# Stores of the first three output chunks: other shares of their odd rows for the sixteen DMA engines

## The chip, the cores and the metric

The kernel runs on one core of a Trainium2 chip. The metric is the device time of one execution in microseconds (us), the median of three runs. Transfers between the chip's memory (HBM) and the core's on-chip memory run on 16 DMA engines, numbered 0 to 15. A transfer is issued by an engine's instruction stream, here by SyncE's (SP) or by GpSimd's (POOL), and is cut into packets on some or all of the 16 engines.

## The reference

Linear attention, a norm of each row, and a soft mixture of experts on its output, all in float32:

```python
kv = np.einsum('bhsd,bhse->bhde', k, v)
out = np.einsum('bhsd,bhde->bhse', q, kv)
x = out / np.sqrt(np.mean(out * out, axis=-1, keepdims=True) + 1e-06) * g_norm   # then rows of B*S by H*D
logits = x @ phi
d = softmax(logits, axis=0)
slot_input = (d.T @ x).reshape(E, S_per_e, D)
slot_out[e] = np.maximum(slot_input[e] @ w1[e], 0.0) @ w2[e]      # for each of 8 experts
result = softmax(logits, axis=1) @ slot_out.reshape(n_slots, D)
```

q, k and v are 8 batches of 8 heads of 576 by 64; there are 8 experts of 4 slots each, with w1 of 512 by 1024 and w2 of 1024 by 512. The output has 4608 rows of 512.

## The kernel before, in words

The program is a list of instructions that is written out in order; a small planner (`Order`) adds the semaphore waits that data make necessary. TensorE builds kv for each batch, then makes the 36 tiles of the attention's output one after another; ScalarE, VectorE and GpSimd norm them and make logits and exponentials. After the last tile come the experts: `expert_h` reads w1, `expert_y` reads w2, and `output` multiplies the combine weights with the slots' results.

All inputs arrive by large transfers of 128 partitions on SP's queue, in the order in which they are used. The last two are weights: one of 4 MB and, behind it, `load_w("w2", 7)` of 2 MB (line 1001). Their places in the on-chip arena are taken by output chunks afterwards.

The output is made in 12 chunks (`n` from 0 to 11; six for each half of the columns). A chunk is a tile of 128 partitions with 1536 numbers each, so one row of one chunk is 6,144 bytes. ScalarE copies the first half of a chunk from PSUM to the arena, VectorE the second. `OUT_ROWS` groups the chunks for the stores: 0 to 2, 3 to 5, 6 and 7, 8 to 11. The last three groups are one transfer each, of 128 partitions, issued from SP when the last chunk of the group is there; each DMA engine takes eight rows of them.

The chunks 0 to 2 are stored otherwise, by the table `FIRST` (line 56), which is all that the change touches, beside `STEPS` (line 61). An entry reads (issuing engine, first row, step between rows, number of rows, pieces `a`, cuts of a row `c`, first chunk, chunk behind the last one). The entry's rows leave as one transfer as soon as its last chunk is there. The table is laid out for this division: with `a` = 1 and 32 or 64 rows a transfer is spread evenly over all 16 DMA engines; with `a` > 1 and rows uncut (`c` = 1) it is cut over `a` engines, on SP's queue the engines 0 to a - 1, on GpSimd's queue the `a` engines that are next in turn; with `c` = 3 it goes to one engine. GpSimd's turn is meant to start at engine 0 and to move on with each transfer by the number of engines that it used. `step_over(n)` is a tiny transfer of n rows of two runs of 16 bytes, which is there to move the turn on by n engines:

```python
    def step_over(n):
        ends = [x[:n, : 2 * w].rearrange("p (c n) -> p c n", c=2)[:, :, :4] for x, w in ((stepped, 8), (first_in, 64))]
        nc.gpsimd.dma_start(*ends)
```

All its calls write the first n rows of one small tile, `stepped`. The first call stands ahead of the experts (line 984); in `store_first` another follows each transfer of GpSimd's while `STEPS`, read from its end, has a number left:

```python
                getattr(nc, engine).dma_start(dst, src)
                if engine == "gpsimd" and steps:
                    step_over(steps.pop())
```

When an instruction writes where a transfer writes, the planner makes it wait until that transfer has landed (`settle`, line 189). At the end SP waits for all the stores.

Of the kernel before, what the change touches and what calls it, by code (L numbers as in the profile page):

```python
# [53 lines left out]
OUT_ROWS = ((0, 1, 2), (3, 4, 5), (6, 7), (8, 9, 10, 11))  # L54
CHUNK = 4 * 12 * 32
FIRST = (
    ("sync", 1, 4, 30, 5, 1, 0, 1), ("sync", 121, 4, 2, 3, 3, 0, 1),
    ("gpsimd", 1, 4, 24, 2, 1, 1, 2), ("gpsimd", 97, 4, 8, 2, 1, 1, 2),
    ("sync", 3, 4, 32, 1, 1, 0, 2), ("sync", 0, 2, 64, 1, 1, 0, 3), ("sync", 1, 2, 64, 1, 1, 2, 3),
)  # L60
STEPS = (7, 6)
SHARED = (5, 11)
BEHIND = {4: (2, 3), 5: (4, 5, 6, 7)}
HEAD = 144
# [224 lines left out]
def soft_moe_linear_attention(nc, first_in, kv_in, q0_in, q1_in, kv4_in, kv5_in, t3_in, w_in, out):  # L289
# [637 lines left out]

    steps = list(STEPS[::-1])

# [169 lines left out]
```

## Time and profile before

| | |
|---|---|
| median of 3 runs | 171.88 us (171.85 to 172.44) |
| the profiled execution's own time | 171.79 us |
| its span, first to last instruction | 170.5 us |
| granted TensorE clock over the span | 0.978 |
| DMA: packets, bytes, mean rate | 4221, 71.65 MB, 420 GB/s |
| queue of SP, share of the 16 engines' span | 97.8% |
| TensorE, ScalarE, VectorE, GpSimd busy | 88%, 52%, 51%, 35% |

The profile's page and the views of its trace come from one execution; their times are microseconds from the first instruction. The profiled execution took 1.3 us more than its span and lies 0.09 us below the median. The share of a DMA queue is the time of its packets over the time of 16 engines, so 100% means that all sixteen moved data throughout.

### The profile page before, as it was taken

The page shows a single profiled execution, that of the slowest core. Times are in us where ns is not written, and L with a number is a line of the kernel's source. Part 1 is how long each engine was busy: PE and PEld are TensorE (multiplying, and loading weights), DVE is VectorE, ACT ScalarE, POOL GpSimd, SP SyncE. Part 2 cuts the span into 40 slices and gives each one's busy share as a digit, 9 for nine tenths or more (in the row PEclk, how much of TensorE's full clock was granted, in tenths as well). Part 3 has the DMA queues.
Part 4 walks back from the last instruction along what each step waited for, and adds up shares of the span by engine and source line. Part 5 has one row for each costly group of instructions (what it writes and reads, how often), then busy time and mean ns, then how long its engine had stood idle before and what let it go on. Part 6 is the DMA issues. An engine that isn't in the chain of part 4 may idle for free.

```text
span 170.5 us, 4241 instructions
## 1 busy us (share of the span) xinstructions
PE 149.4 (88%) x1836; PEld 104.3 (61%) x1836; DVE 86.8 (51%) x185; ACT 88.8 (52%) x230; POOL 59.6 (35%) x73
## 2 busy tenths in 40 slices
PE   7988698989999899999899998989999989989200
PEld 3467587979778878897688683346656633545000
DVE  1122137284677266762946598833888236318300
ACT  3036467795985886859758874102222134418300
POOL 7000707738367745477382778500000004000000
PEclk9999999999999999999999999999999999999965
DMA  5999999999999999999999999999999999999996
GB/s 181 420 444 418 443 409 438 467 416 451 458 419 417 445 441 423 419 400 467 400 465 392 452 404 425 432 452 406 431 431 442 436 442 392 423 409 444 419 450 288
DMA packets 4221, 71.65 MB, mean 420 GB/s; under 512 B 774, under 2 KB 774, under 8 KB 906
## 3 DMA queue, kind: packets, MB, share of 16 engines
q1 hardware_dynamic: 3850, 71.18, 97.8%
q8 instruction: 14, 0.23, 0.5%
q0 software_dynamic: 352, 0.20, 0.4%
q14 instruction: 5, 0.04, 0.1%
HBM read 61.94 MB, written 9.44 MB: 419 GB/s over the span
## 4 chain that ended last, share of the span: by engine, by line
PE 59%; DMA 14%; ACT 12%; DVE 6%; SPq 2%; issue 1%
PE psum L215 59%; DMA arena<-in_kv_dram 14%; ACT bd L215 3%; ACT sq L215 3%; ACT xall L215 2%; SPq L215 2%; DVE logits L215 1%; DVE ms L215 1%; ACT part L215 1%; ACT arena L215 1%; ACT d L215 1%; DVE part L215 1%; ACT r L215 1%; DVE acc L215 1%; DVE r L215 0%
## 5 line engine op out<-in xcount | busy, mean ns | idle before, releaser
L215 PE MATMUL psum<-bd,arena 128*128 128x192 f32 (+1 forms) x320 | 56.1, 335 | 2.1 <-ACT bd L215 1.5
L215 PEld LDWEIGHTS psum<-bd,arena 128*128 128x128 f32 (+1 forms) x320 | 45.4, 179 | 9.0 <-ACT bd L215 2.8
L215 DVE TENSOR_REDUCE ms<-sq 128x16 f32<-128x1024 f32 (+1 forms) x19 | 22.1, 1162 | 32.7 <-ACT sq L215 32.4
L215 POOL TENSOR_TENSOR part<-part,r 128x512 f32<-128x512 f32 x17 | 17.8, 1047 | 49.8 <-DVE r L215 49.8
L215 POOL TENSOR_TENSOR xall<-xall,r 128x512 f32<-128x512 f32 x34 | 34.7, 1042 | 0.0
L215 ACT ACTIVATE sq<-psum 128x512 f32<-128x512 f32 x36 | 21.5, 597 | 10.9 <-PE psum L215 10.7
L215 PEld LDWEIGHTS psum<-arena 128*64 128x64 f32 (+1 forms) x640 | 18.9, 137 | 8.1 <-DMA arena<-in_kv_dram 3.5
L215 PE MATMUL psum<-arena 128*64 128x64 f32 (+1 forms) x640 | 21.4, 226 | 2.6 <-DMA arena<-in_kv_dram 2.4
L215 ACT COPY xall<-psum 128x512 f32<-128x512 f32 x34 | 20.7, 607 | 0.0
L215 ACT COPY part<-psum 128x256 f32<-128x256 f32 (+1 forms) x38 | 13.6, 359 | 8.6 <-DVE part L215 7.5
L215 DVE TENSOR_REDUCE logits<-part 128x64 f32<-128x512 f32 (+1 forms) x18 | 17.8, 990 | 0.0
L215 PE MATMUL psum<-arena,xall 128*32 128x256 f32 x256 | 14.9, 380 | 0.0
L215 DVE COPY arena<-psum 128x768 f32<-128x768 f32 (+1 forms) x12 | 10.5, 889 | 6.8 <-PE psum L215 6.8
L215 ACT COPY arena<-psum 128x768 f32<-128x768 f32 (+1 forms) x14 | 10.2, 754 | 7.1 <-PE psum L215 7.1
L215 PE MATMUL psum<-logits,part 32*128 32x384 f32 x96 | 12.7, 527 | 0.6 <-ACT arena L215 0.4
L215 PE MATMUL psum<-arena,sq 128*32 128x256 f32 x224 | 12.7, 379 | 0.2 <-DVE sq L215 0.2
L215 POOL DMA_DIRECT2D out_dram<-arena x2 | 1.2, 589 | 33.3 <-DVE arena L215 33.3
L215 PEld LDWEIGHTS psum<-arena,xall 128*32 128x32 f32 x256 | 8.1, 110 | 6.3 <-issue 0.9
L215 PE MATMUL psum<-xall,d 128*32 128x258 f32 x144 | 10.8, 390 | 0.9 <-ACT d L215 0.9
L215 ACT COPY bd<-psum 64x128 f32<-64x128 f32 (+1 forms) x32 | 9.9, 308 | 1.6 <-PE psum L215 1.4
L215 PEld LDWEIGHTS psum<-arena,sq 128*32 128x32 f32 x224 | 7.2, 110 | 5.1 <-DVE sq L215 0.5
L215 ACT COPY kvT<-psum 128x256 f32<-128x256 f32 (+1 forms) x9 | 3.1, 348 | 12.0 <-PE psum L215 12.0
(80 smaller groups left out, 128.6 us busy)
## 6 DMA issues: line engine op xcount, KB each, us to landing
arena<-in_w_dram SPq DMA_DIRECT2D x4, 4096.0 KB, 23.3
arena<-in_w_dram SPq DMA_DIRECT2D x4, 2048.0 KB, 19.9
arena<-in_kv_dram SPq DMA_DIRECT2D x3, 2304.0 KB, 23.4
arena<-in_t_dram SPq DMA_DIRECT2D x1, 6912.0 KB, 35.7
arena<-in_w_dram SPq DMA_DIRECT2D x2, 3072.0 KB, 22.5
arena<-in_kv_dram SPq DMA_DIRECT2D x1, 4608.0 KB, 42.6
arena<-in_kv_dram SPq DMA_DIRECT2D x1, 3584.0 KB, 32.2
out_dram<-arena SPq DMA_DIRECT2D x1, 3072.0 KB, 10.7
```

The lines of the kernel that those rows point to most:

```text
L215: inst = getattr(engine, method)(*args, **kwargs)
```

## The change

Only the two tables change. The code that reads them is the same, on the device and in the arrangement of the output.

```diff
 FIRST = (
-    ("sync", 1, 4, 30, 5, 1, 0, 1), ("sync", 121, 4, 2, 3, 3, 0, 1),
-    ("gpsimd", 1, 4, 24, 2, 1, 1, 2), ("gpsimd", 97, 4, 8, 2, 1, 1, 2),
-    ("sync", 3, 4, 32, 1, 1, 0, 2), ("sync", 0, 2, 64, 1, 1, 0, 3), ("sync", 1, 2, 64, 1, 1, 2, 3),
+    ("gpsimd", 121, 4, 2, 3, 3, 0, 2), ("gpsimd", 89, 4, 8, 2, 1, 0, 2), ("gpsimd", 73, 4, 4, 3, 3, 0, 3),
+    ("sync", 0, 2, 64, 1, 1, 0, 3), ("sync", 3, 4, 32, 1, 1, 0, 3), ("sync", 1, 4, 18, 9, 1, 0, 3),
+    ("sync", 89, 4, 6, 3, 1, 2, 3), ("sync", 113, 4, 4, 3, 3, 2, 3),
 )
-STEPS = (7, 6)
+STEPS = (4, 2, 6)
```

Counted in rows of one chunk (6,144 bytes), this is what each DMA engine stores of the chunks 0 to 2 by the tables:

| engines | before: even part + own share | after: even part + own share | difference |
|---|---|---|---|
| 0 | 20 + 12 | 18 + 12 | -2 |
| 1, 2 (each) | 20 + 6 | 18 + 8 | 0 |
| 3 | 20 + 6 | 18 + 6 | -2 |
| 4 | 20 + 6 | 18 + 10 | +2 |
| 5, 6 (each) | 20 + 0 | 18 + 6 | +4 |
| 7, 8 (each) | 20 + 12 | 18 + 14 | 0 |
| 9 to 14 (each) | 20 + 0 | 18 + 0 | -2 |
| 15 | 20 + 4 | 18 + 12 | +6 |

On SP's queue the stores stand behind the last two loads of weights. The piece shows these stores before (-) and after (+), where `32x4608` is 32 rows of three chunks, `9x2x4608` two such rows for each of nine engines and `3x4x512` four rows cut in three.

```order
-L215 DMA out_dram<-arena 5x6x1536
-L215 DMA out_dram<-arena 3x2x512
-L215 DMA out_dram<-arena 32x3072
 L215 DMA out_dram<-arena 64x4608
-L215 DMA out_dram<-arena 64x1536
+L215 DMA out_dram<-arena 32x4608
+L215 DMA out_dram<-arena 9x2x4608
+L215 DMA out_dram<-arena 3x2x1536
+L215 DMA out_dram<-arena 3x4x512
 L215 DMA out_dram<-arena 128x4608
```

The first store on SP's queue was one of chunk 0; now it is the one of 64 rows, which needs chunk 2. Two transfers of the even part became one.

GpSimd's last instructions, in the same way, with the waits that the planner adds; `stepped<-in_first_dram` is `step_over`, `dma_1048` is the landing of the first `step_over`, and `dma_1321` that of the second.

```order
-L215 DMA stepped<-in_first_dram 7x2x4
-L215 DMA out_dram<-arena 2x12x1536 [waits done_scalar,done_vector]
-L215 DMA stepped<-in_first_dram 6x2x4 [waits dma_1048]
-L215 DMA out_dram<-arena 2x4x1536
+L215 DMA stepped<-in_first_dram 4x2x4
+L215 DMA out_dram<-arena 3x2x1024 [waits done_scalar,done_vector]
+L215 DMA stepped<-in_first_dram 2x2x4 [waits dma_1048]
+L215 DMA out_dram<-arena 2x4x3072
+L215 DMA stepped<-in_first_dram 6x2x4 [waits dma_1321]
+L215 DMA out_dram<-arena 3x4x1536 [waits done_scalar,done_vector]
```

There are now three `step_over` transfers, and the third waits for the second to land; behind it on GpSimd stands the store of the four rows for engine 15. TensorE, VectorE and ScalarE have the same instructions in the same order as before.

## Rows read from the trace of the kernel before

**Rows 1.** The page: span; the queue that fetches instructions (packets, MB, share).

```profile
span 170.5 us, 4241 instructions
...
q8 instruction: 14, 0.23, 0.5%
```

**Rows 2.** Stretches: engines' busy time, clock, DMA share, GB/s.

```profile
144.30:168.50 24.20, 13.81 (x164) 6.94 (x164) 7.88 (x11) 7.49 (x12) 0.00 (x0) 0.88 1.01 428
160.00:168.00 8.00, 0.00 (x0) 0.00 (x0) 0.00 (x0) 0.00 (x0) 0.00 (x0) 0.68 1.02 439
```

**Rows 3.** Timeline: TensorE's wait for the last weights; the last copy.

```profile
149.47 1.46 PEld L215 LDWEIGHTS psum<-arena,xall 128*32 128x32 f32 x32 [0.27 <-DMA arena<-in_w_dram]
...
159.12 0.48 ACT L215 COPY arena<-psum 128x384 f32<-128x384 f32 x1 [0.34 <-PE psum L215]
```

**Rows 4.** Timeline: DMA issues on SP, the first load and the stores.

```profile
0.74 0.38 SPq L215 DMA_DIRECT2D arena<-in_first_dram  x1
...
140.22 0.94 SPq L215 DMA_DIRECT2D out_dram<-arena  x1
...
143.20 0.50 SPq L215 DMA_DIRECT2D out_dram<-arena  x1
...
149.06 0.36 SPq L215 DMA_DIRECT2D out_dram<-arena  x1
155.57 0.34 SPq L215 DMA_DIRECT2D out_dram<-arena  x1
```

**Rows 5.** Stretch with the first data packet: columns as in rows 2.

```profile
1.60:1.75 0.15, 0.15 (x2) 0.01 (x1) 0.15 (x2) 0.15 (x1) 0.00 (x0) 1.00 0.58 65
```

**Rows 6.** DMA packets of 140.8:141.9, 141.9:143.85, 143.85:144.3.

```profile
DMA packets 26, 0.49 MB, mean 447 GB/s; under 512 B 6, under 2 KB 6, under 8 KB 6
DMA packets 40, 0.66 MB, mean 336 GB/s; under 512 B 5, under 2 KB 5, under 8 KB 5
DMA packets 21, 0.26 MB, mean 583 GB/s; under 512 B 5, under 2 KB 5, under 8 KB 5
```

**Rows 7.** DMA packets of 168.5:168.7, 168.7:169.7, 169.7:170.05, 170.05:170.2.

```profile
DMA packets 4, 0.02 MB, mean 123 GB/s; under 512 B 3, under 2 KB 3, under 8 KB 3
DMA packets 13, 0.25 MB, mean 246 GB/s; under 512 B 3, under 2 KB 3, under 8 KB 3
DMA packets 9, 0.00 MB, mean 0 GB/s; under 512 B 9, under 2 KB 9, under 8 KB 9
DMA packets 1, 0.00 MB, mean 0 GB/s; under 512 B 1, under 2 KB 1, under 8 KB 1
```

**Rows 8.** Rate in 40 slices of 151.5:151.53, 151.68:151.72, 152.58:152.6, 152.55:152.57.

```profile
GB/s 0 0 0 0 0 0 0 0 0 43 0 0 0 0 0 0 0 8192 0 0 5 0 0 0 0 0 0 0 5 0 0 0 0 0 0 0 5 0 0 0
GB/s 0 0 0 0 0 0 0 0 0 0 0 0 0 0 32 0 0 0 36 0 6144 0 0 12288 0 0 0 0 0 0 0 0 0 0 0 0 0 0 0 0
GB/s 0 0 0 0 8 0 0 0 0 0 0 0 0 0 0 0 8 0 0 0 0 0 0 0 0 0 0 0 64 0 0 0 0 0 0 0 0 0 0 0
GB/s 0 0 8 0 0 0 0 0 0 0 0 0 16 0 0 0 0 0 0 0 0 0 0 0 12288 0 0 0 0 0 0 0 0 0 0 0 0 0 0 0
```

**Rows 9.** Timeline: two of the DMA issues on GpSimd.

```profile
142.25 0.61 POOL L215 DMA_DIRECT2D out_dram<-arena  x1 [33.26 <-DVE arena L215]
142.85 0.56 POOL L215 DMA_DIRECT2D stepped<-in_first_dram  x1
```

**Rows 10.** DMA issues of GpSimd: KB each, us from issue to landing.

```profile
stepped<-in_first_dram POOLq DMA_DIRECT2D x1, 0.2 KB, 6.0
...
stepped<-in_first_dram POOLq DMA_DIRECT2D x1, 0.2 KB, 12.3
```

**Rows 11.** GpSimd's queue in 145.95:146.1: packets, MB, share.

```profile
q0 software_dynamic: 4, 0.01, 10.9%
```

**Rows 12.** DMA packets of 157.64:157.72.

```profile
DMA packets 8, 0.07 MB, mean 922 GB/s; under 512 B 3, under 2 KB 3, under 8 KB 3
```

## The prediction

> **What bounds the kernel now.** I read the stretches first. From 144.3 to 168.5 us the DMA engines are busy for 1.01 of their time at 428 GB/s, and from 160 to 168 for 1.02 at 439, while every other engine stands still [rows 2]. The last copy of an output chunk starts at 159.12 and takes 0.48 [rows 3]; the span lasts until 170.5 [rows 1]. So the end is set by sixteen queues of bytes, and within them by the engine that is done last. Two things can move it: that engine's bytes, and time in which it stands idle.
>
> Which engine is last is read from the tiny packets. When an engine has written its share of a transfer of SP's queue it writes one packet of 4 bytes, and the windows of DMA packets count these as "under 512 B". For the last store, three engines are done between 168.5 and 168.7, three between 168.7 and 169.7, nine between 169.7 and 170.05, and one behind 170.05 [rows 7]; I call that last one 170.1. With the middle of each group the mean is about (3 x 168.6 + 3 x 169.2 + 9 x 169.9 + 170.1) / 16 = 169.5. A perfect division of the bytes could thus save 0.6 us, 0.35% of the time. This bounds what new shares alone can give.
>
> The order among the engines is older than the stores. For the 4 MB load, before any store has reached the engines, six have their mark between 140.8 and 141.9, five between 141.9 and 143.85, and five between 143.85 and 144.3 [rows 6]. The last five are 2 to 3 us behind the first. I take part of it to be fetches of instructions: 14 packets fill 0.5% of 16 engines' span [rows 1], so one takes about 0.005 x 170.5 x 16 / 14 = 1 us of one engine, and the changed kernel's TensorE program, by far the longest, is the same. So I expect this pattern again.
>
> **The five late engines.** 428 GB/s over 16 engines is 26.75 GB/s for one, and a row of a chunk (6,144 bytes) takes 0.23 us. From its mark at about 144.0 an engine without a share of its own still has 131,072 bytes of weights and 20 + 24 + 16 + 32 = 92 rows to move, 696,320 bytes or 26.0 us, and is done at 170.0. That is where the late end marks lie. Six rows more would put it at 171.4, which no engine reaches. So the five late engines are among the eight that have no share of their own now: 5, 6 and 9 to 14.
>
> Which five? GpSimd's `step_over(6)`, between its two stores, touches the engines 9 to 14: six engines show a packet of 32 bytes (two runs of 16), the others one of 8. In slices so small that rate times time gives a packet's size, three of 32 bytes (43 GB/s x 0.75 ns, then 32 and 36 GB/s x 1 ns, the second with a mark of 4 bytes beside it) stand between 151.5 and 151.72. The late five pass this point about a microsecond later, as 1.4 us of lag asks: one packet of 32 bytes (64 GB/s x 0.5 ns) between 152.58 and 152.6, and one of 8 (16 x 0.5) just before [rows 8]. So three of the engines 9 to 14 are not late, three at most are, and **both 5 and 6 belong to the late five**. Even without this reading, five drawn from these eight miss both 5 and 6 in only 6 of 56 ways.
>
> **The change part by part.** The bytes in all are the same. Per row 0.23 us: engines 9 to 14, 0 and 3 give up two rows and end 0.46 earlier; 1, 2, 7 and 8 keep theirs; 4 gets two (+0.46), 5 and 6 get four each (+0.92), 15 gets six (+1.38). The even part's transfer that falls away, and the new transfers, are priced within these rows.
>
> Engines 5 and 6 lie between 169.8 and 170.1 now [rows 7]; I take 169.95. They end at 170.87, between 170.7 and 171.0. Engines 9 to 14 end at 170.1 - 0.46 = 169.64 at the latest. Engine 4 is at 170.1 + 0.46 = 170.6 at worst and 169.1 at best, as nothing in the rows says which of the remaining it is. The unchanged ones stay at or under 170.1.
>
> Engine 15 has four rows of its own now, and with them can't be one of the late five. I take it as one of the three that are done by 168.7 [rows 7], since its lag of that time, 141.5 + 26.0 + 0.9, fits there. With six rows more: 168.6 + 1.38 = 170.0.
>
> **The new wait.** The third `step_over` waits on GpSimd until the second has landed; behind it only engine 15's twelve rows are queued, and nobody but SP's last wait needs them. The second will be issued about where the one of 142.85 stands [rows 9]. That one took 12.3 us to land, the first, in quiet, 6.0 [rows 10]: 148.9 to 155.2. I take 153, nearer to the row that has the same place. Two issues of 0.6 later, 3.7 us pass from issue to first packet (142.25 to 145.95 [rows 9, 11]): engine 15's rows start at about 157.3, between 153 and 160. They need 12 x 0.23 = 2.8 us and have until 170. So the wait is hidden by engine 15's other stores, as long as those don't run dry. They do, a little: without its four rows and with two even rows less, engine 15 is through chunks 3 to 5 six rows earlier than the first engines now, 157.7 - 1.4 = 156.3 [rows 12], while SP issues the next store at 155.57 [rows 4]. The first load's packets came 1.0 us after its issue (0.74 to 1.75 [rows 4, 5]), so that store begins at 156.6: 0.3 idle, at most 1.0 until its late rows fill the gap. Engine 15: 170.3, at most 171.0.
>
> **Later stores.** SP's first store now waits for chunk 2, to 143.20 instead of 140.22 [rows 4]. It costs nothing, as the first engines (mark at 141.0) have 4.9 us of weights left, until 145.9, and 143.20 + 1.0 lies before that; without this cover each microsecond of delay would be one of idle time on all engines. SP's five issues, 0.5 to 0.9 each, end by 147, before the issue of 149.06 [rows 4]. TensorE waits for the last weights until 149.47 [rows 3]; GpSimd's packets appear at 145.95 [rows 11], when engines 7 and 8 are at the end of those weights; if they delayed them, the cost would be at most the 0.5 us of two of its rows. Fewer, longer rows: the share of 1.01 leaves nothing to gain.
>
> The same share of 1.01 [rows 2] says that a transfer's start and end are hidden behind its neighbours, so one more store and one more `step_over` cost 0, and the sum holds 0 for them. The Trainium skill (DMA: Bandwidth & Descriptors, section Anatomy of one DMA — SWDGE (gpsimd) path) fits a transfer as 2.0 us plus its bytes over 436 GB/s, mostly a wait for the last write's receipt. By that rule the two would add 4.0 us if they stood in line, and the estimate would be 176.6 instead of 172.6.
>
> **The sum.** The last mark goes from 170.1 to 170.87, +0.77. On the profiled execution's 171.79 us that is 172.56; the median of the runs lies 0.09 higher. I say 172.6, with 172.3 to 172.9 for this case (5 and 6 between 170.7 and 171.0, engine 15 up to 171.0, the 0.09). Against 171.88 it is 0.4% slower; 0.5% (0.86 us) is about what a measurement of this kernel can tell from no change.
>
> **The rivals.**
> First, the wait costs more (slower): engine 15's rows come so late that they stick out. The point is a landing of the second `step_over` later than 171 - 2.8 - 3.7 - 1.2 = 163.3, that is 20 us after its issue; each microsecond behind it is one on the end. For it speaks that 6.0 grew to 12.3 under load; against it, that 20 is far off. A landing at 165 gives 174.3.
> Second, the shares land on other engines: nothing in the rows shows where a store of GpSimd's cut in three goes. Twelve rows on engine 14 instead of 15 end at 169.64 + 2.8 = 172.4: 174.1. The Trainium skill (DMA: Bandwidth & Descriptors, section Why a DMA increments its semaphore by 16 and not by 1) gives one engine for two counts without a common divisor, but adds that some copies of GpSimd's go to all 16 by partitions instead; no run here shows which holds for this shape.
> Third, starts are not hidden: two more transfers, each with 1.0 us from issue to first packet, in line: 174.6. Against it stands the share of 1.01.
> Fourth, the lag of the engines differs from run to run, and 5 and 6 are not late in the new one: then 15 or 4 is last at 170.0 to 170.6, no change: 171.7 to 172.3.
> Fifth, the balance works as the table of shares might suggest: everything near 169.6, 171.3.
>
> **How the numbers follow.** Forecast 0.63, first rival 0.10, second 0.06, third 0.03, fourth 0.14, fifth 0.04. The range reaches from 171.6 to 173.0: it leaves out the fifth, the second and third and most of the first, about 0.2. Slower by over 0.5% means over 172.74: a fifth of the forecast's cases (0.13) and the first three (0.19), 0.32. Faster by over 0.5% would need more than a perfect division gives: 0.03. The rest, 0.65, is within 0.5%.
>
> **What would show it.** In the new trace the last store's marks should lie at 169.4 to 169.6 for several engines and near 170.9 for two. GpSimd should issue its last store ten microseconds after the one before. SP's stores should begin at 143.2, with a DMA share near 1.0 through 168. Two marks near 170.0 and none later would mean that the lag of 5 and 6 is not a fixed one; an end mark alone behind 171 would point at engine 15.

## The result and the profile after

| | before | after |
|---|---|---|
| median of 5 runs each, one chip | 171.85 us (171.74 to 172.44) | 174.04 us (173.93 to 174.41) |
| ratio, 95% interval | 1 | 1.0117 [1.0097, 1.0137] |
| profiled execution: time, span | 171.79, 170.5 us | 173.93, 172.6 us |
| granted clock over the span | 0.978 | 0.967 |

The change makes the kernel slower by 1.2%. The forecast of 172.6 us had the sign, but the time lies 1.0 us above the range of 171.6 to 173.0.

The page of the changed kernel, with its span and the first row of the DMA queues:

```profile
span 172.6 us, 4242 instructions
...
DMA packets 4292, 71.65 MB, mean 415 GB/s; under 512 B 915, under 2 KB 915, under 8 KB 951
## 3 DMA queue, kind: packets, MB, share of 16 engines
q1 hardware_dynamic: 3777, 71.18, 96.6%
```

The bytes are the same as before; SP's queue fills 96.6% of the sixteen engines' span instead of 97.8%. The stretches of [rows 2], in the changed kernel:

```profile
144.30:168.50 24.20, 13.59 (x164) 6.77 (x156) 7.66 (x11) 7.49 (x12) 1.22 (x2) 0.85 1.01 425
160.00:168.00 8.00, 0.00 (x0) 0.00 (x0) 0.00 (x0) 0.00 (x0) 0.00 (x0) 0.58 1.03 439
```

Up to 168.5 the DMA engines are as full as they were (1.01, then 1.03). The lost time is behind that. The end marks of the last store, as in [rows 7], in the windows 168.9 to 169.95 and 169.95 to 172.3 (the second with its rate in 40 slices):

```profile
DMA packets 17, 0.05 MB, mean 47 GB/s; under 512 B 15, under 2 KB 15, under 8 KB 15
...
GB/s 0 0 0 0 0 0 0 418 0 0 0 0 0 0 0 0 0 0 0 0 0 0 418 0 0 0 0 0 0 0 0 0 0 0 0 0 0 0 0 0
DMA packets 3, 0.05 MB, mean 21 GB/s; under 512 B 1, under 2 KB 1, under 8 KB 1
...
q1 hardware_dynamic: 3, 0.05, 4.9%
```

Fifteen engines have their mark before 169.95, earlier than the last one of [rows 7] (170.1). One has two packets of 24,576 bytes left that start at 170.4 and 171.3 (418 GB/s x 0.0588 us each), and its mark comes at 172.2. It moves data all the time: 4.9% of 16 engines for 2.35 us are 1.84 us, which is two such packets. So in this execution a single engine carries the whole loss of 2.1 us (172.2 against 170.1). Followed back packet by packet it is the engine with GpSimd's twelve rows, by the table engine 15. An end mark alone behind 171 is what the prediction named as the sign of engine 15.

GpSimd's DMA issues in the changed kernel (start, duration, and in brackets the idle time ahead and what ended it), and behind them the landing of the second `step_over` in the view of DMA issues (KB, us from issue to landing):

```profile
142.03 0.64 POOL L215 DMA_DIRECT2D out_dram<-arena  x1 [33.49 <-DVE arena L215]
142.66 0.59 POOL L215 DMA_DIRECT2D stepped<-in_first_dram  x1
143.23 0.58 POOL L215 DMA_DIRECT2D out_dram<-arena  x1
152.19 0.57 POOL L215 DMA_DIRECT2D stepped<-in_first_dram  x1 [8.38 <-DMA stepped<-in_first_dram]
152.84 0.65 POOL L215 DMA_DIRECT2D out_dram<-arena  x1
```

```profile
stepped<-in_first_dram POOLq DMA_DIRECT2D x1, 0.1 KB, 9.2
```

The new wait is there, where it was expected: 8.38 us of GpSimd, ended by the second `step_over` at 152, 9.2 us after its issue. The store for engine 15 is issued at 152.84. The packets of 156.74 to 159.0 and of 159.0 to 161.25, with GpSimd's queue (q0):

```profile
DMA packets 305, 0.93 MB, mean 411 GB/s; under 512 B 241, under 2 KB 241, under 8 KB 248
...
q0 software_dynamic: 233, 0.04, 12.0%
...
DMA packets 77, 0.92 MB, mean 407 GB/s; under 512 B 0, under 2 KB 0, under 8 KB 5
...
q0 software_dynamic: 5, 0.03, 6.1%
```

Packets between 2 and 8 KB are engine 15's rows: 248 - 241 = 7 in the first window and 5 in the second, twelve in all. In the second window nothing else is on q0, and 6.1% of 16 x 2.25 us is 2.2 us: these five rows fill the whole of one engine, at 0.44 us each. All twelve take from 156.74 to 161.25, 4.5 us instead of the 12 x 0.23 = 2.8 of the prediction.

Could it be engine 14, as in the second rival, whose 172.4 and 174.1 lie close to what was measured? No: an engine's packets of the third `step_over` stand ahead of the rows on GpSimd's queue, and it has six rows (`STEPS` is used from its front: 4, 2, 6), one of 32 bytes for each of the engines 9 to 14. From 153.1 on nothing is on q0 until two packets right ahead of the first row, in the window 156.72 to 156.744 (40 slices of 0.6 ns):

```profile
GB/s 0 0 0 0 0 0 0 0 13 0 0 0 0 0 0 0 0 0 0 0 0 0 0 0 0 0 0 0 0 0 0 0 0 0 0 7 0 0 0 0
```

They have 13 x 0.6 = 8 and 7 x 0.6 = 4 bytes, so the engine with the rows is none of 9 to 14.

A second loss lies earlier. These are two windows of 4 ns each, around the first packet of chunks 3 to 5 on engine 15 (from 150.272), and around one of another engine (from 150.284):

```profile
q1 hardware_dynamic: 2, 0.02, 2348.4%
...
q1 hardware_dynamic: 1, 0.02, 1071.9%
```

The share divides a packet's whole time by the window, so the second packet took 10.719 x 16 x 0.004 = 0.69 us and the first, with a mark of 4 bytes, 1.50. Both have 18,432 bytes. Without its own rows engine 15 had come to the end of its queue, and the first packet of the new store met it dry for about 0.8 us: the packet ended at 151.77, so its data came at about 151.77 - 0.69 = 151.1, some 2.2 us after the issue at 148.84. The prediction reckoned with 1.0, from the first load's issue to the start of its first packet [rows 4, 5]. That packet took long, too. The windows 1.746 to 1.75 and 3.505 to 3.509 of the kernel before hold one packet of this load each:

```profile
q1 hardware_dynamic: 1, 0.01, 2193.8%
...
q1 hardware_dynamic: 1, 0.01, 575.0%
```

That is 1.40 us for the first, which starts at 1.75, and 0.37 for the later one. By the same reckoning the first load's data came at about 1.75 + 1.40 - 0.37 = 2.8, which is 2.0 us after its issue. So the 1.0 left out most of a first packet's time. The rows of SP for the issue at 148.84, for the two ahead of it, and the last copy of a chunk:

```profile
145.54 2.25 SPq L215 DMA_DIRECT2D out_dram<-arena  x2
148.84 0.36 SPq L215 DMA_DIRECT2D out_dram<-arena  x1
...
158.90 0.48 ACT L215 COPY arena<-psum 128x384 f32<-128x384 f32 x1 [0.34 <-PE psum L215]
```

The compute engines are not late: the last copy starts at 158.90, against 159.12 in [rows 3].

### The profile page after: what moved, and what is told of

It is laid out like the page before. It is cut to its first block, busy times and chain, and to the rows that moved or that the text cites. A ratio compares the mean times of both kernels' runs of the same rounds, so it can differ in the third digit from the quotient of the medians.

```text
span 172.6 us, 4242 instructions
## 1 busy us (share of the span) xinstructions
PE 148.7 (86%) x1836; PEld 104.2 (60%) x1836; DVE 86.8 (50%) x185; ACT 88.8 (51%) x230; POOL 60.9 (35%) x75
## 3 DMA queue, kind: packets, MB, share of 16 engines
q1 hardware_dynamic: 3777, 71.18, 96.6%
## 4 chain that ended last, share of the span: by engine, by line
PE 59%; DMA 13%; ACT 12%; DVE 6%; SPq 1%; issue 1%
PE psum L215 59%; DMA arena<-in_kv_dram 13%; ACT bd L215 3%; ACT sq L215 3%; ACT xall L215 2%; DVE logits L215 1%; SPq L215 1%; DVE ms L215 1%; ACT part L215 1%; ACT arena L215 1%; ACT d L215 1%; DVE part L215 1%; ACT r L215 1%; DVE acc L215 1%; DVE r L215 0%
## 5 line engine op out<-in xcount | busy, mean ns | idle before, releaser
L215 POOL DMA_DIRECT2D out_dram<-arena x3 | 1.9, 621 | 33.6 <-DVE arena L215 33.5
```

The lines of the kernel that those rows point to most:

```text
L215: inst = getattr(engine, method)(*args, **kwargs)
```

## The experiments

Two theories stood against each other. By the first, engine 15 sets the end: its rows are late (the wait) and slow. By the second, the lag of engines 5 and 6 with four rows more each sets it, as forecast. In the expectations, A is the late store and B the slow rows (both of engine 15), C the wait by itself, D the engines 5 and 6, and E engine 15 without them. Rivals to both: the other form of the even part, the wait by itself, and the place of the rows in the arena. Every kernel here computes the whole output.

**The change without its wait.** The `step_over` calls write different columns of `stepped` in turn. Against the changed kernel:

```diff
+        at = 4 * (turns[0] % 2)
+        turns[0] += 1
-        ends = [x[:n, : 2 * w].rearrange("p (c n) -> p c n", c=2)[:, :, :4] for x, w in ((stepped, 8), (first_in, 64))]
+        ends = [
+            x[:n, : 2 * w].rearrange("p (c n) -> p c n", c=2)[:, :, i : i + 4]
+            for x, w, i in ((stepped, 8, at), (first_in, 64, 0))
+        ]
```

> The change, with every second step_over writing other columns of its small tile, so that the third no longer waits for the second to land; shares, order and bytes are the same. Theory A (the late store): engine 15's twelve rows came at 156.7 us, after its other stores had run dry, and this lateness cost the 2.2 us; without the wait they reach the engine near 148, its last mark falls from 172.2 to 170.0 or 170.3, and the kernel takes 171.4 to 172.0 us. Theory B (the share): twelve short rows on engine 15 are too slow whenever they come; its mark stays behind 171.5 and the kernel takes 173.3 us or more.

Measured: 173.40 us (172.98 to 174.29), ratio 1.0091 [1.0069, 1.0114]. GpSimd's five issues follow each other without a pause; the last one, the store for engine 15, in its timeline:

```profile
145.11 0.66 POOL L215 DMA_DIRECT2D out_dram<-arena  x1
```

The wait is worth 0.64 us (174.04 - 173.40), less than a third of the loss; by the two ratios, each against its own runs of the kernel before, it is 0.45, and their intervals overlap. Engine 15's rows now lie between 150.37 and 154.44 with no dry time ahead, but they are still slow: 4.07 us. The last of them, in a window of 10 ns from 153.84, and the marks of the last store behind 170.26, both from the view of DMA packets:

```profile
q0 software_dynamic: 1, 0.01, 374.4%
...
DMA packets 5, 0.02 MB, mean 22 GB/s; under 512 B 4, under 2 KB 4, under 8 KB 4
```

That row took 3.744 x 16 x 0.01 = 0.60 us. Engine 15 is done at 170.84, 1.35 us earlier than with the wait: 0.8 of dry time and 0.43 of the rows' time account for 1.2 of it. In this execution, two marks come later than its own, at 171.01 and 171.25; followed packet by packet they belong to engines 5 and 6. So both theories hold here, one behind the other: once engine 15 is earlier, 5 and 6 end last.

**Half of engine 15's rows**, with the wait kept; the other six go to engines 0 and 1:

```diff
-("gpsimd", 73, 4, 4, 3, 3, 0, 3),
+("gpsimd", 73, 4, 2, 3, 3, 0, 3),
+("sync", 81, 4, 2, 2, 1, 0, 3),
```

> The change with the wait left in, and only two of the four partitions on engine 15 (six rows instead of twelve); the other two go to the engines 0 and 1 on SP's queue, three rows each more (0.7 us). Theory A: the late store costs what it takes alone on the engine; in the changed kernel twelve packets took 4.5 us, so six take 2.3, engine 15's mark falls by 2.2 to 170.0, and the kernel takes 171.6 to 172.2 us. Theory B, with the same slow packets, gives the same. Theory C (the wait itself sticks out, whatever hangs on it): the time stays at 173.5 or more.

Measured: 172.96 us (171.94 to 173.50), ratio 1.0058 [1.0038, 1.0078], 1.1 us less than the change. Six late rows took 2.32 us here, 0.39 each; engine 15 is still last, at 170.94, in the profiled execution. This is neither the 171.6 to 172.2 that was expected of A and B (engine 15 done at 170.0) nor the 173.5 of C. The kernel also gives SP a sixth store to issue: the store of chunks 3 to 5 is issued at 149.85, 0.5 us behind its last copy, while in the changed kernel it was 0.03.

**The wait alone.** The kernel before, with its `step_over(6)` cut into one of 2 and one of 4:

```diff
-                    step_over(steps.pop())
+                    n_over = steps.pop()
+                    step_over(2)
+                    step_over(n_over - 2)
```

> The kernel before, with its second step_over cut into two (2 and 4 engines), so that the second of them waits for the first to land, as in the change; shares are those of before. The last store of GpSimd's, four rows each on engines 15 and 0, comes some 9 us later. Theory A: engine 15 had 1.4 us to spare and four rows take 0.9 to 1.5 us; the engines 0 and 15 end at most 0.7 us later, and the kernel takes 171.8 to 172.5 us. Theory C (the wait itself costs 2 us): 173.5 us or more.

Measured: 171.88 us (171.64 to 172.47), ratio 1.0001 [0.9987, 1.0014]. GpSimd waits longer than in the changed kernel, and the store behind it is issued at 155.24:

```profile
154.65 0.59 POOL L215 DMA_DIRECT2D stepped<-in_first_dram  x1 [10.82 <-DMA stepped<-in_first_dram]
155.24 0.56 POOL L215 DMA_DIRECT2D out_dram<-arena  x1
```

A wait of 10.82 us costs nothing when only four rows for each of the engines 0 and 15 stand behind it. It is the share behind the wait that makes it count.

**The even part alone**, in the kernel before:

```diff
-    ("sync", 3, 4, 32, 1, 1, 0, 2), ("sync", 0, 2, 64, 1, 1, 0, 3), ("sync", 1, 2, 64, 1, 1, 2, 3),
+    ("sync", 0, 2, 64, 1, 1, 0, 3), ("sync", 3, 4, 32, 1, 1, 0, 3), ("sync", 1, 4, 32, 1, 1, 2, 3),
```

> The kernel before, with only its even part in another form: the 32 rows of the chunks 0 to 2 as one transfer behind the 64 rows, and chunk 2 of the other 32 rows by itself; every engine stores the same bytes as before. All theories: no change, 171.6 to 172.1 us. A fixed time of each transfer, or one saved by longer rows, would show as a difference of 0.5 us or more.

Measured: 171.80 us (171.70 to 172.74), ratio 1.0002 [0.9990, 1.0014]. Rows of three chunks at once neither cost nor save, as the prediction had it.

**The share of 5 and 6 alone.** The kernel before, with the store of chunk 0 cut over seven engines instead of five. Engines 5 and 6 get four rows more, as in the change, and 1 to 4 two fewer:

```diff
-    ("sync", 1, 4, 30, 5, 1, 0, 1), ("sync", 121, 4, 2, 3, 3, 0, 1),
+    ("sync", 1, 4, 28, 7, 1, 0, 1), ("sync", 113, 4, 4, 3, 3, 0, 1),
```

> The kernel before, with only its first transfer (chunk 0) cut over seven engines in place of five: the engines 5 and 6 get four rows (0.92 us) that they did not have, the engines 1 to 4 have two fewer; no other wait, no new transfer. Theory D (5 and 6 are among the late engines in most executions, as three of the eight engines without a share are not in any one of them): the last mark goes from 170.1 to 170.9 in most executions, and the kernel takes 172.3 to 172.9 us. Rival E (all the loss of the change is engine 15's, and 5 and 6 have time to spare): 171.6 to 172.0 us.

Measured: 172.59 us, +0.69 on the 171.90 of before, ratio 1.0033 [1.0020, 1.0047]. The runs fall into two groups: ten of twelve lie between 172.37 and 173.10, two at 171.77 and 171.80. The profiled execution is one of the two. Its packets of 168.4 to 170.2 and of 170.2 to 171:

```profile
DMA packets 26, 0.29 MB, mean 164 GB/s; under 512 B 14, under 2 KB 14, under 8 KB 14
...
DMA packets 0, 0.00 MB, mean 0 GB/s; under 512 B 0, under 2 KB 0, under 8 KB 0
```

No mark stands behind 170.2, although 5 and 6 have their four rows more: they were not late in that execution. In the others the time fits 0.77, the price of the prediction; none of them has a trace, so that 5 and 6 ended last there is argued.

**The change without engine 15's share**; engines 0 to 3 get the twelve rows from SP. Run twice, the second time beside the last two kernels below:

```diff
-("gpsimd", 73, 4, 4, 3, 3, 0, 3),
+("sync", 73, 4, 4, 4, 1, 0, 3),
```

> The change without engine 15's own share: its four partitions go to the engines 0 to 3 on SP's queue, three rows each; the wait stays, with nothing behind it. Rival E: engine 15's late mark is gone, nothing else is later than 170.3, and the kernel takes 171.6 to 172.2 us. Theory D: the shares of 5 and 6 are left, and so are about 0.8 to 1.1 us: 172.4 to 173.0 us.

> The change without engine 15's own share once more, as its six runs lay in two groups (172.6 to 172.8 and 173.7 to 174.4) and the one with a trace had a lower granted clock between 20 and 40 us. What the shares of 5 and 6 leave is 172.4 to 173.0 us; a median of 173.5 or more would say that another loss sits in the change, beside the engines 5, 6 and 15.

Measured: 173.24 us (172.56 to 174.38), ratio 1.0081 [1.0051, 1.0111], and again 173.07 (172.56 to 174.16), ratio 1.0080 [1.0053, 1.0107]. Six of the twelve runs lie at 172.56 to 172.79, where the theory of 5 and 6 puts them; the others reach from 173.36 to 174.38. The profiled executions are the slowest of each six. Stretches of the first one (columns as in [rows 2]), and behind them SP's first six stores, its store of chunks 3 to 5, and the last copies of these chunks:

```profile
18.00:20.00 2.00, 1.81 (x52) 1.81 (x54) 0.00 (x0) 0.14 (x1) 2.00 (x3) 0.84 1.22 518
20.00:26.00 6.00, 5.51 (x48) 4.85 (x44) 0.00 (x0) 1.63 (x5) 0.67 (x1) 0.50 0.96 409
146.00:148.00 2.00, 2.00 (x29) 0.95 (x32) 1.73 (x2) 0.92 (x2) 0.02 (x1) 1.00 0.92 340
152.00:154.00 2.00, 1.58 (x29) 0.76 (x22) 0.29 (x1) 0.21 (x1) 0.00 (x0) 1.00 0.74 273
```

```profile
145.19 7.30 SPq L215 DMA_DIRECT2D out_dram<-arena  x6
...
152.59 0.37 SPq L215 DMA_DIRECT2D out_dram<-arena  x1
...
149.84 1.18 ACT L215 COPY arena<-psum 128x768 f32<-128x768 f32 x2 [1.92 <-PE psum L215]
```

Two of these stretches in the changed kernel:

```profile
20.00:26.00 6.00, 5.51 (x60) 4.57 (x56) 2.10 (x3) 3.79 (x11) 0.62 (x1) 1.00 0.96 408
152.00:154.00 2.00, 1.91 (x19) 0.92 (x18) 0.80 (x2) 0.83 (x2) 1.22 (x2) 1.00 1.03 426
```

In this execution TensorE had the lower of its two levels, 1.2 GHz (0.50), from 20 to 26 us; the 0.84 of the stretch from 18 to 20, in which it was busy for 1.81 us, says that it fell at about 19.4. The changed kernel's had 2.4 there. The second profiled execution shows the same fall. The compute is then 2 us later up to the end, and SP's first store comes at 145.19 instead of 142.97. That is behind the point where the engines reach the end of the weights: share 0.92 at 146 to 148. This is the lost cover that the prediction named for the first store.

The second gap, 0.74 at 152 to 154, has a further cause. SP's six stores, one more than in the change, took 7.30 us to issue, up to 152.49. The last copy of chunks 3 to 5 ended at 149.84 + 1.18 = 151.02, but their store was issued at 152.59, 1.6 us later. At the usual clock, with a first store at 142.97, six issues would last until about 150.3 and that copy would end at 148.81, as in the changed kernel (an estimate from these rows). So giving the twelve rows to SP is likely to delay that store in every execution, and these runs don't show the shares of 5 and 6 by themselves.

Nor does the clock explain all six later runs: the two with a trace have a mean of 0.950 and 0.952, the other four 0.960 to 0.973, and the six early runs 0.968 to 0.976. What makes those four later is open. Runs of the kernel before at a mean clock of 0.955 or 0.956 lie 0.4 to 0.9 us above the median of their set; its first store needs chunk 0 alone [rows 4].

**Other rows for engine 15**, without the wait: rows 1 to 13 of the chunks instead of 73 to 85, SP's rows moved up.

```diff
-("gpsimd", 73, 4, 4, 3, 3, 0, 3),
-("sync", 1, 4, 18, 9, 1, 0, 3),
+("gpsimd", 1, 4, 4, 3, 3, 0, 3),
+("sync", 17, 4, 18, 9, 1, 0, 3),
```

> The change without the wait, and engine 15's four partitions taken from the other end of the arena (1 to 13 in place of 73 to 85; the rows of the engines 0 to 8 move up by four). If the place of the rows makes engine 15's packets slow (340 to 380 ns on average in place of 234), they are at 234 here, engine 15 ends 1.3 us earlier, and the kernel takes up to 0.5 us less than 173.4. If not, the packets are as slow as before and the time is 173.2 to 173.6 us.

Measured: 173.18 us (173.01 to 173.76), ratio 1.0079 [1.0063, 1.0095], the same as without the move within the intervals. Engine 15's rows took 3.5 us instead of 4.07: the first eight 0.23 each, the last four up to 0.56. The place explains a part at most, and each figure is of one execution.

**5 and 6 spared**, without the wait, engine 15 with six rows. The whole table, in place of the changed one:

```diff
+    ("gpsimd", 121, 4, 2, 3, 3, 0, 2), ("gpsimd", 65, 4, 14, 2, 1, 0, 2), ("gpsimd", 41, 4, 2, 3, 3, 0, 3),
+    ("sync", 0, 2, 64, 1, 1, 0, 3), ("sync", 3, 4, 32, 1, 1, 0, 3), ("sync", 65, 4, 16, 1, 1, 2, 3),
+    ("sync", 1, 4, 10, 5, 1, 0, 3), ("sync", 49, 4, 4, 4, 1, 0, 3),
```

> Both suspects taken out of the change: no wait, the engines 5 and 6 without a share, engine 15 with six rows in place of twelve; the rows go to an even transfer of 16 rows of chunk 2 (one row for each engine), to 0 to 3 and to 4, 7 and 8 (29, 33 and 33 rows in all). The even part is then 19 rows. If the lateness of 15 and the shares of 5 and 6 are the whole loss, it takes 171.6 to 172.2 us. If GpSimd's third store or the five stores on SP's queue cost by themselves, 172.5 us or more.

Measured: 172.38 us (172.03 to 172.97), ratio 1.0033 [1.0022, 1.0045], a little above what was expected. With 15 and 5, 6 out of the way, the engines 0 to 3 end last (170.47 and 170.61 in the profiled execution); three of them had got two rows more than before. 1.7 of the 2.2 us of the change's loss are gone, and the kernel before is still ahead.

**Late against early, with 5 and 6 spared.** Twelve rows for engine 15 in both; the first has the wait, the second the `stepped` columns in turn as above. Against the kernel of the last test:

```diff
-("gpsimd", 41, 4, 2, 3, 3, 0, 3),
-("sync", 49, 4, 4, 4, 1, 0, 3),
+("gpsimd", 41, 4, 4, 3, 3, 0, 3),
+("sync", 57, 4, 2, 2, 1, 0, 3),
```

> Engine 15 alone: twelve rows of its own on GpSimd's queue, behind the wait, as in the change, but the engines 5 and 6 without a share (19 rows on each of the eight engines 5, 6, 9 to 14; 28 on 0 and 1, 25 on 2 and 3, 29 on 4, 33 on 7 and 8, 31 on 15). Theory A (engine 15's late rows set the change's time): its mark is at 172.2 to 172.5 again, the others at or under 170.6, and the kernel takes 173.8 to 174.4 us. If instead the shares of 5 and 6 were needed for the loss: 172.0 to 172.8 us.

> The same shares, without the wait. In the change without its wait, engine 15's mark came 1.3 us earlier: it no longer stood dry for 0.8 us near 150.3, and its short rows took 4.1 us in place of 4.5. So its mark is near 171.1 here, and the kernel takes 172.4 to 173.0 us, 1.0 to 1.5 us less than with the wait. If the wait costs nothing for itself, both take the same.

Measured: late 173.26 us (172.91 to 174.20), ratio 1.0087 [1.0068, 1.0107]; early 172.73 (172.63 to 172.87), ratio 1.0051 [1.0038, 1.0064]. The wait costs 0.53 here and 0.64 above (by the ratios 0.62 and 0.45), and here the intervals lie apart. Six rows more on engine 15, early, cost 0.35 (172.73 - 172.38) although their bytes alone are 1.4 us: engine 15 had some 1 us of room there. Lateness takes 0.5 of it away. The late kernel came out 0.5 below the lower end of what the theory of engine 15 gave.

## Why the prediction was wrong, by its own steps

**What bounds the kernel** was right. Sixteen queues of bytes end the span, and the engine that is done last sets the time. The limit of 0.6 us for any division was not put to a test: no table tried came under the kernel before.

**The step that failed** is "engine 15: 170.3, at most 171.0". It ended at 172.19. Of its terms:

- "They need 12 x 0.23 = 2.8 us" was mis-sized: 4.5 us in the changed kernel, 4.07 without the wait. The 0.23 is right for a row that SP's queue moves in a full stretch, and for most of GpSimd's uncut rows; a row in this store of GpSimd's took 0.38 on average (4.5 / 12), and 0.34 without the wait. That is 1.7 us.
- The idle time was put at the wrong place and too low. I looked at 156.6, between chunks 3 to 5 and the next store; there the late rows closed the gap. The gap was one store earlier, at 150.3, where engine 15 had neither its rows nor anything else, and it was 0.8 us, since data came 2.2 us after an issue and not 1.0. The 1.0 was misread: it ends where the first load's first packet starts [rows 4, 5], and data came about 2.0 us after that issue.
- 170.0 + 1.7 + 0.8 = 172.5, against 172.2: the start at 168.6 may have been 0.3 high.

Once the late rows have begun they hold the engine: twelve packets lie back to back while the store of chunks 6 and 7, issued at 155.34, waits behind them until 161.25. The Trainium skill (DMA: Bandwidth & Descriptors, section Queues, rings and completion order) says that an engine drains a whole packet of one queue, typically nine to seventeen descriptors, before it switches to another; if each row of the trace is one descriptor, the twelve go together by that rule, and in this store the trace agrees. In another it does not: of GpSimd's store for two engines, ahead of it, packets of 12,288 bytes start on one engine at 147.04, 148.18 and 149.32, 1.14 us apart, so that a packet of SP's (0.69) lies between two of its own (0.46). So engine 15's late share was not mixed into the other bytes here; that it never is, no run shows.

**The wait** was right in place, length and contents (153 predicted, 152 measured; the run of the wait alone cost nothing). It was wrong to call it hidden: it shifts 4.5 us of one engine's work behind a hole, and costs 0.5 to 0.6. So the first rival's result came (174.3 against 174.04), but by luck and not by its mechanism, which needs a landing behind 163.3: it was at 152.

**The late engines** were right in size and wrong in constancy. The share of 5 and 6 alone costs 0.69, against 0.77 predicted, and by the times in ten of twelve runs. But in the changed kernel's own profiled execution all engines except 15 were done by 169.95. That is the premise of the fourth rival. "I expect this pattern again" was the weak sentence: one execution was read as the rule. The forecast of 172.6 is what six of the twelve runs without engine 15's share gave (172.56 to 172.79), but that kernel has the delayed store as well.

**The second rival** is ruled out, though its 174.1 is as close as the first rival's figure: the store cut in three went to one engine, and to none of 9 to 14. The Trainium skill (DMA: Bandwidth & Descriptors, section Why a DMA increments its semaphore by 16 and not by 1) gives one engine for two counts without a common divisor, and the trace agrees with it. **The third rival** and the estimate of 176.6 beside it are ruled out: one more small transfer and another form of the even part cost nothing in a full queue (1.0001 and 1.0002), and with both new transfers fifteen engines were done by 169.95.

**The cover of the first store** held at the usual clock (first store at 142.97, share 1.01), and the price that was named without it came due when TensorE was 2 us late. SP's issues were under-priced: the last two of the five took 2.25 us together and ended at 147.8, not 147. It cost nothing here, ahead of the issue at 148.84; with a sixth store it delayed that issue.

**Open:** why engine 15's rows are slow. GpSimd's queue and the lateness are not enough. In the run of the wait alone, seven of the eight late rows of the engines 15 and 0, which are not cut in three, lie in the window 157.9 to 158.65:

```profile
DMA packets 54, 0.32 MB, mean 426 GB/s; under 512 B 29, under 2 KB 29, under 8 KB 36
...
q0 software_dynamic: 32, 0.04, 15.5%
```

These are 36 - 29 = 7 rows and 25 tiny packets, which took 15.5% of 16 x 0.75 us = 1.86 us together, so at most 0.27 for a row on average. (The eighth, the first of them, took 0.67.) The cut in three, by which one engine takes the whole store, is not enough either: the first such store of the changed kernel has six pieces of 4,096 bytes, and each took 0.16 us, which is 0.23 for 6,144 bytes. Another place in the arena gave 3.5 us for twelve rows against 4.07, and lateness 4.5 against 4.07, in single executions. What lowers the clock in some executions is open as well.

## What to carry to other kernels

When work is balanced over queues that are already full, price a late share by the engine's whole schedule: what it has to move at each gap before the share comes, and how long these packets take on that queue, not by bytes alone. A helper transfer that writes a buffer again puts a landing of 9 to 12 us under load in series; here it was free for four rows an engine and not for twelve. And before shares are fitted to engines that run late, look at more than one execution: a lag that moves from run to run can't be balanced away.

## What the runs showed of the hardware

- Rows of 6,144 bytes in a store of GpSimd's that goes to one engine took 0.29 to 0.39 us on average in seven kernels, single ones up to 0.62, against 0.23 for the shortest ones in the same store; uncut rows of GpSimd's, as late, took at most 0.27 on average (seven of eight).
- From issue to data on SP's queue: about 2.0 us for the first load and 2.2 us for the store at 148.84, where the first packet took 1.40 and 1.50 us in place of 0.37 and 0.69.
- SP's issue of a store took 0.36 us for the 128 rows at 148.84, and 1.0 to 1.3 for each of the three stores ahead of it. Shape is not all: an issue of 128 rows right behind six others took 1.23 (the run with half of engine 15's rows).
- Which engines end last changes between executions: with four rows more each, 5 and 6 ended last at 171.01 and 171.25 in the change without its wait, while in the kernel before with that share alone no mark lay behind 170.2.
